# Feed-forward products: one PSUM tile of two banks becomes two tiles of one bank

## The chip, the core and the metric

The kernel runs on one core of a Trainium2 chip. The metric is device time in microseconds of one execution. The engines have short names here: PE is the matrix engine (its weight loads are shown apart, as PEld), DVE the vector engine, ACT the scalar engine, POOL the GpSimd engine and SP the engine that issues most of the transfers. Every engine works through its own list of instructions in order; semaphores make one engine wait for another. PSUM is the memory that PE writes its products to; here it is used as 8 banks of 512 float32 values on each of 128 partitions.

## The reference

```
q_pool = q.reshape(B, H, S // 2, 2, D).mean(axis=3)         # B 4, H 8, S 1152, D 64
scores = (q_pool @ k.T) / sqrt(D);  attn = softmax(scores)
x = (attn @ v), heads side by side                            # 2304 x 512
h = x @ w_in                                                  # 2304 x 2048
g = h * tanh(softplus(h))                                     # Mish
out = g @ w_out                                               # 2304 x 512, float32
```

The first half is an attention with pooled queries, the second a feed-forward layer with Mish between two matrix products. The change touches the second half alone.

## The kernel before

The attention fills the first part of the program and leaves its result transposed in SBUF, in `xT`. The feed-forward layer then works on three blocks of 768 tokens (`tp` 0, 1, 2), and in each on pairs of 128-wide slices of the hidden dimension (`fp` 0 to 7). One pair (block, slice pair) is a unit, written `(tp, fp)`; names in the trace carry no such numbers. Both matrix products are done by a seven-product (Winograd form of Strassen) scheme, and each float32 product as three passes over rounded parts: high by high, high by low, low by high. So one product of the scheme is a few groups of three matmuls of 128x384.

In a unit, `HP` (line 616 of the profile) makes the seven products of the first matrix, 42 matmuls, into PSUM tiles `ma`, `mb`, `mc` of a pool of their own. DVE and ACT combine them and apply Mish, and ACT and POOL split the results into high and low parts (`Gh`, `Gl`, `GhT`, `GlT`).

`OP(u, i, m)` (line 679) makes product `i` (1 to 7) of the second matrix for half `m` (0 or 1) of 128 output rows each: 14 groups of three matmuls, 42 in all. Products 1, 6, 7 and 4 form a chain: each is added in PSUM to what the one before left there. They share the tile `OA`, which is allocated once per unit as `[P, 2, 512]`, two banks, where half `m` uses bank `m`. After each step of the chain `EO(u, i, m)` (line 692, on DVE; in the first units of a block on ACT, line 690) adds the sum of that moment to the output in `xT`. Products 5, 3 and 2 use one-bank tiles with tags `x` (half 0) and `pv` (half 1).

In block 0 most units use a plain product, `OT` (line 732, groups of six matmuls of 128x512), whose six results are evicted by `EV` (line 740). Results 0 and 1, and 3 and 4, share a two-bank tile with the tag `Mb`; results 2 and 5 use `pv`. The last unit uses `OZ` (line 711) and `EZ` (line 716), with one bank of `Mb`, `x` and `pv` in turn. The tag `x` also holds a step of the weight conversion, `conv` (line 359).

The order in which each engine gets its instructions is written out by hand: tables of times (`FILL`, `EDGE`, `STEADY`) are sorted and issued in that order. No scheduler moves anything. What the tile framework adds are the waits: it tracks which tile an instruction reads or writes, and gives an instruction a semaphore wait where a tile's earlier reader or writer is on another engine.

Of the kernel before, what the change touches and what calls it, by code (L numbers as in the profile page):

```python
# [8 lines left out]
F32 = mybir.dt.float32  # L9
# [6 lines left out]
PSUM = bass.MemoryType.PSUM  # L16


def f32(ap):
    return ap.bitcast(F32)  # L20
# [3 lines left out]
def tile_pooled_attention_then_winograd_ffn(ctx: ExitStack, tc: tile.TileContext, q, k, v, moe_w_in, moe_w_out, out, outT):  # L24
# [3 lines left out]
    NT, DM = B * SQ, out.shape[1]  # L28
    DFF = moe_w_out.shape[0]
    P = 128  # L30
# [13 lines left out]
    TH = TW // 2  # L44
# [16 lines left out]
    pools, shut = {}, {}  # L61

    def open_pool(name, bufs, side="left", space=bass.MemoryType.SB):
        shut[name] = ExitStack()
        pools[name] = shut[name].enter_context(
            tc.tile_pool(name=name, bufs=bufs, side=side, space=space, reuse_waits="tile")
        )
        return pools[name]
# [3 lines left out]
    if True:  # L72
# [16 lines left out]
        dram = open_pool("dram", 1, space=bass.MemoryType.DRAM)  # L89
# [11 lines left out]
        ps1 = open_pool("ps1", 1, side="right", space=PSUM)  # L101
# [209 lines left out]
        wraw, wt, cw, cl, ws = {}, {}, {}, {}, {}  # L311
        wS, wO, wf = {}, {}, {}
# [24 lines left out]
        def conv(n, m):  # L337

            f, io = pieces[n]
            x = wraw[n]  # L340
            if n not in wt:
                wt[n] = wraw_p.tile([P, DM], F32, tag="wt", name=f"wt{n}") if n < 4 else w32((0, n // 4), n % 4)
            if n < 4 and 0 < m < 4:
                z = wt[n].bitcast(U16).rearrange("p (m two) -> p m two", two=2)
                u = x.bitcast(U16)
                if m == 1:
                    act.activation(z[:, :, 0], u[:, :, 1], AF.Copy, bias=2.0**-14 - 0.5, scale=2.0**-13)
                elif m == 2:
                    pool.tensor_scalar(z[:, :, 1], u[:, :, 3], 32768.0, 32768.0, ALU.is_ge, ALU.mult)
                else:  # L350
                    w = wt[n].bitcast(I32)
                    dve.scalar_tensor_tensor(
                        w, in0=cw[n].bitcast(I32), scalar=3, in1=w, op0=ALU.logical_shift_left, op1=ALU.bitwise_or
                    )
                return
            if n > 7:
                w, a = wt[n].bitcast(I32), x[:, :, 1]
                if m == 0:
                    cw[n] = ps1.tile([P, DM], F32, tag="x", name=f"cw{n}")
                    act.activation(cw[n], f32(a), AF.Copy, scale=2.0**-112)  # L360
                elif m == 1:
                    cl[n] = pools["psW"].tile([P, DM], I32, tag="cl", name=f"cl{n}")
                    act.activation(cl[n], x.bitcast(U16)[:, :, 1], AF.Copy, bias=2.0**-14 - 0.5, scale=2.0**-13)
                elif m == 2:
                    dve.scalar_tensor_tensor(w, in0=a, scalar=-(2**31), in1=cl[n], op0=ALU.bitwise_and, op1=ALU.bitwise_or)
                else:
                    dve.scalar_tensor_tensor(
                        w, in0=cw[n].bitcast(I32), scalar=3, in1=w, op0=ALU.logical_shift_left, op1=ALU.bitwise_or
                    )
                    load_w(n + 2)  # L370
                    sp.dma_start(out=spill[n], in_=wt[n])
                return
            if m == 0:
                cw[n] = wt[n] if n > 3 else ps1.tile([P, DM], F32, tag="x", name=f"cw{n}")
                act.activation(cw[n], f32(x[:, :, 1]), AF.Copy, scale=2.0**-112)
                return
            w = cw[n].bitcast(I32)
            if m == 1:
                dve.tensor_scalar(w, w, 3, None, ALU.logical_shift_left)
            elif m == 2:  # L380
                dve.scalar_tensor_tensor(
                    w, in0=x[:, :, 1], scalar=-(2**31), in1=w, op0=ALU.bitwise_and, op1=ALU.bitwise_or
                )
            elif m == 3:
                dve.scalar_tensor_tensor(
                    wt[n].bitcast(I32), in0=x[:, :, 0], scalar=29, in1=w, op0=ALU.logical_shift_right, op1=ALU.bitwise_or
                )
                load_w(n + 2)
                sp.dma_start(out=spill[n], in_=wt[n])
            elif m == 4:  # L390
                ws[f, io] = [pools["w0"].tile([P, DM], F32R, tag=f"{t}{io}{f}", name=f"w{t}{io}_{f}") for t in "hl"]
                act.copy(ws[f, io][0], wt[n])
                sp.dma_start(out=spill[n], in_=wt[n])
            else:
                hi, lo = ws[f, io]
                pool.tensor_tensor(lo, wt[n], f32(hi), ALU.subtract)
# [23 lines left out]
        hs, gs, os_, ch = {}, {}, {}, {}  # L420
# [243 lines left out]
        CHAIN_O = (1, 6, 7, 4)  # L664

        def OP(u, i, m):
            q, s, g = PROD[i]
            wh, wl = (x[:, s, m * P:(m + 1) * P] for x in weights(u, q))
            gh, gl = gs[u, g]
            if i == 1 and m == 0:  # L670
                o = ps1.tile([P, 2, 512], F32, tag="Mb", name=f"OA{u[0]}_{u[1]}")
                os_[u, "A"] = o[:, :, 0:TH]
            if i in CHAIN_O:
                o = os_[u, "A"][:, m]
            else:
                o = ps1.tile([P, 512], F32, tag=("x", "pv")[m], name=f"O{i}{m}_{u[0]}_{u[1]}")[:, 0:TH]
                os_[u, i, m] = o
            for n, (x, y) in enumerate(((wh, gh), (wh, gl), (wl, gh))):
                pe.matmul(o, x, y, start=(n == 0 and i not in CHAIN_O[1:]), stop=(n == 2 and i not in CHAIN_O[:3]), skip_group_check=True)  # L679

        def EO(u, i, m):
            tp, fp = u
            first = u in FIRST
            if i == 5 and first:
                ex[tp, m] = pools["wq"].tile([P, TH], F32, tag=f"ex{m}", name=f"ex{m}_{tp}")
            h, t = {1: (0, 0), 2: (0, 0), 6: (0, 1), 3: (0, 1), 7: (1, 1), 4: (1, 0), 5: (0, 0)}[i]
            acc = ex[tp, m] if i == 5 else half(tp, h, t)[:, m]
            o = os_[u, "A"][:, m] if i in CHAIN_O else os_[u, i, m]
            if first and (i == 5 or tp == 2 and i in (1, 6, 7, 4)):
                act.copy(acc, o)  # L690
            else:
                dve.tensor_tensor(acc, acc, o, ALU.add)  # L692
# [8 lines left out]

        def OZ(u, n):
            t, c = 1 - n // NKC, n % NKC
            o = ps1.tile([P, 2, 512], F32, tag="Mb", name=f"OZ{n}")[:, 0, 0:TH] if n % 3 == 0 else ps1.tile([P, 512], F32, tag=("x", "pv")[n % 3 - 1], name=f"OZ{n}")[:, 0:TH]
            os_[u, n] = o
            wh, wl = wf[u, "o"]
            for f in range(2):
                g, l = gs[u, 2 * f + t]
                a, b = (w[:, f, c * P:(c + 1) * P] for w in (wh, wl))
                for m, (x, y) in enumerate(((a, g), (a, l), (b, g))):  # L710
                    pe.matmul(o, x, y, start=(f == 0 and m == 0), stop=(f == 1 and m == 2))  # L711
# [6 lines left out]

        def OT(u, n):
            k = (n + KT // 2) % KT  # L720
            if n % 3 == 0:
                o = ps1.tile([P, 2, 512], F32, tag="Mb", name=f"O{u[0]}_{u[1]}_{n}")
                os_[u, n], os_[u, n + 1] = o[:, 0], o[:, 1]
            elif n % 3 == 2:
                os_[u, n] = ps1.tile([P, 512], F32, tag="pv", name=f"O{u[0]}_{u[1]}_{n}")
            o = os_[u, n]
            t, a = divmod(k, KT // 2)
            wh, wl = wf[u, "o"]
            for f in range(2):
                g, l = (x[:, a * P:(a + 1) * P] for x in gs[u, 2 * f + t])  # L730
                for m, (x, y) in enumerate(((g, wh), (g, wl), (l, wh))):
                    pe.matmul(o, x, y[:, f], start=(f == 0 and m == 0), stop=(f == 1 and m == 2))
# [15 lines left out]
        for n, u in enumerate(units):  # L748
            if u[0] == 0:
                banks[u] = ("b", "a", "c") if n % 2 else ("a", "b", "c")  # L750
            else:
                x, y, z = banks[units[n - 1]]
# [6 lines left out]
        def close(*names):  # L759
            for n in names:  # L760
                shut[n].close()
# [9 lines left out]
        def reuse_psH():  # L771
            close("psH")
            open_pool("psW", 1, space=PSUM)

        def reuse_rest():
            close("p3", "p2", "p1")
# [7 lines left out]
        def reuse_lead():  # L784
# [604 lines left out]
            (load_q, -3.5700),  # L1389
        ]  # L1390
        EDGE = [
            (-191.5356, split_h, 1, 1),
            (-182.6058, split_l, 1, 1),
            (-166.9356, split_h, 1, 2),
# [1181 lines left out]
        for _, fn, *a in plan:  # L2576
            fn(*a)
        mode.close()
        close("wq", "g", "sx", "ev", "xt", "pad", "wf", "xp", "wraw", "psW", "ps1", "dram")


SHAPE = (4, 8, 1152, 64)
# [34 lines left out]
```

## Time and profile before

| what | value |
| --- | --- |
| median of 3 runs | 815.39 us (813.95 to 815.86) |
| the profiled execution | 815.27 us, span of its instructions 813.2 us |
| PE busy | 774.7 us, 95% of the span |
| DVE, ACT, POOL busy | 686.3, 642.7, 652.1 us |
| granted PE clock | 0.996 of full speed over the span |

The profiled execution is 0.1 us from the median, and 2.1 us longer than the span of its instructions. Times in rows count from the start of the span. The attention ends and block 0 of the feed-forward layer begins near 455 us; blocks 1 and 2 run from about 570 us to the end. A matmul is shown for 0.34 us when it is 384 columns wide, and the next one starts about 0.17 us after it, so that back to back matmuls overlap in the picture; the idle time in square brackets counts from the end of the one before, and what a stall costs is longer than that idle time by the overlap.

### The profile page before, as it was taken

The page shows a single profiled execution, that of the slowest core. Times are in us where ns is not written, and L with a number is a line of the kernel's source. Part 1 is how long each engine was busy: PE and PEld are TensorE (multiplying, and loading weights), DVE is VectorE, ACT ScalarE, POOL GpSimd, SP SyncE. Part 2 cuts the span into 40 slices and gives each one's busy share as a digit, 9 for nine tenths or more (in the row PEclk, how much of TensorE's full clock was granted, in tenths as well). Part 3 has the DMA queues.
Part 4 walks back from the last instruction along what each step waited for, and adds up shares of the span by engine and source line. Part 5 has one row for each costly group of instructions (what it writes and reads, how often), then busy time and mean ns, then how long its engine had stood idle before and what let it go on. Part 6 is the DMA issues. An engine that isn't in the chain of part 4 may idle for free. (4 is left out here: it accounts for less than half of the span.)

```text
span 813.2 us, 14323 instructions
## 1 busy us (share of the span) xinstructions
PE 774.7 (95%) x5123; PEld 554.9 (68%) x5123; DVE 686.3 (84%) x959; ACT 642.7 (79%) x1110; POOL 652.1 (80%) x505
## 2 busy tenths in 40 slices
PE   6999999999999999999899999999989999899988
PEld 4455455555555554554569888997989989799987
DVE  5999999999999999999858688876677797567666
ACT  6999999999999999999768887776765676765752
POOL 4779998898898898898983987777776788777883
PEclk9999999999999999999999999999999999999999
DMA  7557546546656556555426887856543221433322
GB/s 266 154 157 186 144 133 174 120 135 144 164 141 170 116 138 146 139 139 115 85 50 193 284 287 245 271 174 189 172 160 110 91 92 49 132 112 107 116 98 97
DMA packets 44470, 121.90 MB, mean 150 GB/s; under 512 B 4592, under 2 KB 16368, under 8 KB 44400
## 3 DMA queue, kind: packets, MB, share of 16 engines
q1 hardware_dynamic: 34608, 71.45, 26.6%
q0 software_dynamic: 4608, 28.31, 17.7%
q10 hardware_dynamic: 5184, 21.24, 7.7%
q8 instruction: 40, 0.66, 0.3%
q14 instruction: 30, 0.25, 0.1%
HBM read 70.65 MB, written 22.02 MB: 114 GB/s over the span
## 5 line engine op out<-in xcount | busy, mean ns | idle before, releaser
L164 PE MATMUL s<-qT,kT 64*128 64x288 f32 x1152 | 202.5, 448 | 5.7 <-ACT TA L174 2.9
L164 PEld LDWEIGHTS s<-qT,kT 64*128 64x128 f32 x1152 | 91.8, 186 | 101.1 <-DVE rmax L185 25.4
L174 ACT COPY TA<-s 128x576 f32<-128x576 f32 x192 | 117.7, 638 | 22.4 <-PE s L164 16.0
L223 DVE TENSOR_TENSOR TA<-TA,Mb 128x1152 f32<-128x1152 f32 x96 | 128.9, 1348 | 1.7 <-PE Mb L217 0.8
L246 PE MATMUL pv<-TA,vn 128*64 128x288 f32 x768 | 116.5, 426 | 1.1 <-ACT TA L227 1.1
L227 ACT ACTIVATE TA<-TA 128x1152 f32<-128x1152 f32 x96 | 112.8, 1176 | 4.2 <-DVE TA L223 3.8
L232 POOL TENSOR_TENSOR acc<-TA 128x1152 f32<-128x1152 f32 x32 | 85.1, 2661 | 35.9 <-PE s L164 19.0
L238 POOL TENSOR_TENSOR acc<-acc 128x576 f32<-128x576 f32 x64 | 92.1, 1439 | 3.8 <-DMA acc<-TB 2.6
L185 DVE TENSOR_TENSOR rmax<-s,rmax 128x576 f32<-128x576 f32 x128 | 93.4, 750 | 1.4 <-ACT TB L174 1.2
L246 PEld LDWEIGHTS pv<-TA,vn 128*64 128x64 f32 x768 | 47.7, 138 | 48.8 <-issue 10.5
L692 DVE TENSOR_TENSOR xT<-xT,OA 128x384 f32<-128x384 f32 x104 | 55.0, 550 | 28.0 <-PE OA L679 27.9
L223 DVE TENSOR_TENSOR TB<-TB,Mb 128x1728 f32<-128x1728 f32 x32 | 62.2, 1945 | 0.0
L246 PE MATMUL pv<-TB,vn 128*64 128x288 f32 x384 | 61.3, 415 | 0.0
L174 ACT COPY TB<-s 128x576 f32<-128x576 f32 x96 | 59.8, 654 | 0.8 <-PE s L164 0.8
L598 POOL TENSOR_TENSOR wbl<-wS,wbh 128x1024 fp32r<-128x1024 f32 x20 | 49.6, 2481 | 8.8 <-ACT wbh L594 8.8
L227 ACT ACTIVATE TB<-TB 128x1728 f32<-128x1728 f32 x32 | 52.7, 1648 | 0.0
L185 DVE TENSOR_TENSOR rmax<-s,TA 128x576 f32<-128x576 f32 x64 | 48.4, 756 | 4.2 <-ACT TA L174 4.1
L598 POOL TENSOR_TENSOR wal<-wS,wah 128x768 fp32r<-128x768 f32 x19 | 35.7, 1878 | 19.6 <-ACT wah L594 19.4
L234 POOL TENSOR_TENSOR acc<-TA 128x576 f32<-128x576 f32 x32 | 45.6, 1426 | 1.8 <-ACT TA L227 1.7
L246 PEld LDWEIGHTS pv<-TB,vn 128*64 128x64 f32 x384 | 23.9, 136 | 25.2 <-issue 11.9
L598 POOL TENSOR_TENSOR woal<-wO,woah 128x1024 fp32r<-128x1024 f32 x13 | 31.4, 2417 | 9.8 <-ACT woah L594 8.8
L620 ACT COPY s<-ma 128x384 f32<-128x384 f32 x44 | 21.2, 482 | 20.4 <-PE ma L616 20.4
(305 smaller groups left out, 2246.0 us busy)
## 6 DMA issues: line engine op xcount, KB each, us to landing
acc<-TB POOLq DMA_DIRECT2D x32, 864.0 KB, 6.4
ri<-in_moe_w_in_dram SPq DMA_DIRECT2D x16, 512.0 KB, 4.3
ro<-in_moe_w_out_dram SPq DMA_DIRECT2D x16, 512.0 KB, 4.7
qn<-in_q_dram ACTq DMA_DIRECT2D x12, 576.0 KB, 5.1
kT<-in_k_dram ACTq DMA_DIRECT2D x12, 576.0 KB, 3.8
vn<-in_v_dram ACTq DMA_DIRECT2D x12, 576.0 KB, 4.1
wS<-sumsh SPq DMA_DIRECT2D x12, 512.0 KB, 4.0
wO<-sumso SPq DMA_DIRECT2D x13, 384.0 KB, 4.2
```

The source lines that it names most:

```text
L164: pe.matmul(s[:, j, 0:HQ], kT[64 * j:64 * j + 64, c], qT[64 * j:64 * j + 64, hf], start=True, stop=True,)
L174: act.copy(T(i, c), ss[i, c])
L185: dve.tensor_tensor(ss[i, c] if c == FOLD else r, ss[i, c], x, ALU.max)
L223: dve.tensor_tensor(x, x, Mbs[i].unsqueeze(1).to_broadcast([P, w, W]), ALU.subtract)
L227: act.activation(x, x, AF.Exp, scale=0.0625)
L232: pool.tensor_tensor(accs[i][:, 0:2], T(i, 0, 2), T(i, 2, 4), ALU.add)
L234: pool.tensor_tensor(accs[i][:, 2], T(i, 4), T(i, 5), ALU.add)
L238: pool.tensor_tensor(accs[i][:, 0], accs[i][:, 0], accs[i][:, n - 2], ALU.add)
L246: pe.matmul(pvs[i][64 * j:64 * j + 64, 0:HQ], vn[:, j, c, :], T(i, c)[:, j], start=(pvn[i] == 1), stop=(pvn[i] == NC),)
L598: (dve if e == "dve" else pool).tensor_tensor(l, w_part(u, q), f32(h), ALU.subtract)
L620: act.copy(sv[u, n], ps[u, "c" if n == 2 else "a"])
L692: dve.tensor_tensor(acc, acc, o, ALU.add)
```

## The change

A second PSUM pool, `ps2`, takes the place of `ps1` in the feed-forward layer. It is opened where `ps1` is closed, in `reuse_ps1`, at a place of the `EDGE` table just before the first `OT` products. The two banks of the tag `Mb` become two tags of one bank, `y0` and `y1`; `x` and `pv` stay. Both pools have four banks, so nothing else moves. `OA` is now a list of two tiles, one for each half; `OT` takes `y0`, `y1` and `pv` in turn; `OZ` goes round all four tags where it used three.

```diff
-                o = ps1.tile([P, 2, 512], F32, tag="Mb", name=f"OA{u[0]}_{u[1]}")
-                os_[u, "A"] = o[:, :, 0:TH]
+                os_[u, "A"] = [pools["ps2"].tile([P, 512], F32, tag=t, name=f"OA{t}{u[0]}_{u[1]}")[:, 0:TH] for t in ("y0", "y1")]
             if i in CHAIN_O:
-                o = os_[u, "A"][:, m]
+                o = os_[u, "A"][m]
...
-            o = ps1.tile([P, 2, 512], F32, tag="Mb", name=f"OZ{n}")[:, 0, 0:TH] if n % 3 == 0 else ps1.tile([P, 512], F32, tag=("x", "pv")[n % 3 - 1], name=f"OZ{n}")[:, 0:TH]
+            o = pools["ps2"].tile([P, 512], F32, tag=("y0", "y1", "x", "pv")[n % 4], name=f"OZ{n}")[:, 0:TH]
...
-            if n % 3 == 0:
-                o = ps1.tile([P, 2, 512], F32, tag="Mb", name=f"O{u[0]}_{u[1]}_{n}")
-                os_[u, n], os_[u, n + 1] = o[:, 0], o[:, 1]
-            elif n % 3 == 2:
-                os_[u, n] = ps1.tile([P, 512], F32, tag="pv", name=f"O{u[0]}_{u[1]}_{n}")
+            os_[u, n] = pools["ps2"].tile([P, 512], F32, tag=("y0", "y1", "pv")[n % 3], name=f"O{u[0]}_{u[1]}_{n}")
...
+        def reuse_ps1():
+            close("ps1")
+            open_pool("ps2", 1, side="right", space=PSUM)
...
+            (47.9700, reuse_ps1),
```

The instructions of each engine, and their order, are those of before; what differs is which of them wait, and for what. On DVE in unit (1, 3), before, these are the evictions of product 1, half 0 and half 1, the two instructions behind them, and the evictions of product 6, which share a row because they read alike:

```order
L692 TENSOR_TENSOR xT_60<-xT_60,OA1_3_6762 128x384 [waits DVE_49,PE_49]
L692 TENSOR_TENSOR xT_60<-xT_60,OA1_3_6762 128x384 [waits DVE_49]
L653 TENSOR_TENSOR T4f1_3_6786<-ma1_3_6518,T2f1_3_6719 128x384 [waits Activation_49]
L692 TENSOR_TENSOR ex0_1_6055<-ex0_1_6055,O50_1_3_6780 128x384 [waits PE_49]
L692 TENSOR_TENSOR xT_60<-xT_60,OA1_3_6762 128x384 [waits PE_49] x2
```

The same place with the change:

```order
L691 TENSOR_TENSOR xT_60<-xT_60,OAy01_3_6784 128x384 [waits DVE_49,PE_49]
L691 TENSOR_TENSOR xT_60<-xT_60,OAy11_3_6785 128x384 [waits DVE_49,PE_49]
L653 TENSOR_TENSOR T4f1_3_6809<-ma1_3_6539,T2f1_3_6741 128x384 [waits Activation_49]
L691 TENSOR_TENSOR ex0_1_6074<-ex0_1_6074,O50_1_3_6803 128x384 [waits PE_49]
L691 TENSOR_TENSOR xT_60<-xT_60,OAy01_3_6784 128x384 [waits PE_49]
L691 TENSOR_TENSOR xT_60<-xT_60,OAy11_3_6785 128x384 [waits PE_49]
```

Nothing moved. Before, the second eviction has no wait for PE of its own: the first one already waits until PE has written both halves of the tile. With the change each of the two waits for its own half.

On PE in the same unit, before, these are the two groups of product 7 (half 0, then half 1), which add to the bank that product 6 left:

```order
L679 MATMUL OA1_3_6762<-GhT31_3_6733,woah1_3_6683 128x384 [waits DVE_49]
L679 MATMUL OA1_3_6762<-GlT31_3_6734,woah1_3_6683 128x384 [waits Pool_49]
L679 MATMUL OA1_3_6762<-GhT31_3_6733,woal1_3_6684 128x384
L679 MATMUL OA1_3_6762<-GhT31_3_6733,woah1_3_6683 128x384
L679 MATMUL OA1_3_6762<-GlT31_3_6734,woah1_3_6683 128x384
L679 MATMUL OA1_3_6762<-GhT31_3_6733,woal1_3_6684 128x384
```

The same six with the change:

```order
L678 MATMUL OAy01_3_6784<-GhT31_3_6755,woah1_3_6705 128x384 [waits DVE_49]
L678 MATMUL OAy01_3_6784<-GlT31_3_6756,woah1_3_6705 128x384 [waits Pool_49]
L678 MATMUL OAy01_3_6784<-GhT31_3_6755,woal1_3_6706 128x384
L678 MATMUL OAy11_3_6785<-GhT31_3_6755,woah1_3_6705 128x384 [waits DVE_49]
L678 MATMUL OAy11_3_6785<-GlT31_3_6756,woah1_3_6705 128x384
L678 MATMUL OAy11_3_6785<-GhT31_3_6755,woal1_3_6706 128x384
```

Here too the instructions are the same. Before, the first group waits for DVE once, for the evictions of both halves that stand ahead of it in the program, and the second needs no wait of its own. With the change each half waits for its own bank's eviction.

## Rows read from the trace of the kernel before

**Rows 1.** The page, busy time and its share of the span, by engine
```profile
PE 774.7 (95%) x5123; PEld 554.9 (68%) x5123; DVE 686.3 (84%) x959; ACT 642.7 (79%) x1110; POOL 652.1 (80%) x505
```
**Rows 2.** Busy time by stretch, columns named in its first row
```profile
core 0: us, PE busy (x) PEld busy (x) DVE busy (x) ACT busy (x) POOL busy (x), PEclk, DMA share, GB/s
500.00:560.00 60.00, 59.65 (x297) 53.05 (x295) 47.68 (x75) 43.95 (x83) 47.40 (x39) 1.00 0.69 224
560.00:620.00 60.00, 54.95 (x300) 52.03 (x300) 41.94 (x83) 36.68 (x71) 44.53 (x28) 1.00 0.48 152
620.00:700.00 80.00, 73.86 (x409) 69.99 (x409) 60.74 (x113) 54.54 (x110) 63.49 (x44) 1.00 0.28 93
700.00:780.00 80.00, 73.36 (x409) 70.04 (x408) 56.42 (x116) 51.08 (x102) 63.45 (x43) 1.00 0.36 116
...
638.65:655.05 16.40, 15.07 (x85) 14.47 (x85) 12.62 (x25) 11.47 (x24) 13.52 (x10) 1.00 0.41 132
```
**Rows 3.** Groups of PE instructions, 560 to 814 us, that were waited before
```profile
line engine op names shapes xcount | busy us, mean ns | idle before us <-releasers
...
L679 PE MATMUL OA<-GhT,woah 128*128 128x384 f32 x56 | 21.4, 382 | 15.2 <-DVE xT L692 14.4 <-ACT xT L690 0.6
...
L616 PE MATMUL ma<-T4h,wbh 128*128 128x384 f32 x30 | 10.2, 340 | 0.6 <-DVE mb L624 0.6
...
L732 PE MATMUL O<-woh,Gh 128*128 128x512 f32 x8 | 3.3, 407 | 1.6 <-DVE xT L740 1.6
```
**Rows 4.** Everything on tile OA: durations (min/median/max), and who waited for it
```profile
L692 DVE TENSOR_TENSOR xT<-xT,OA x104: 541/548/555, 574.2 to 799.9; 128x384 f32<-128x384 f32 x104
...
  PE OA L679: 15.6, 23
```
**Rows 5.** Timeline of PE and DVE in unit (1, 3), 638.65 to 642.74 us
```profile
638.65 0.34 PE L679 MATMUL OA<-Gh,woah 128*128 128x384 f32 x1
...
639.52 0.34 PE L679 MATMUL OA<-Gh,woal 128*128 128x384 f32 x1
639.69 0.34 PE L679 MATMUL O<-GhT,woah 128*128 128x384 f32 x1
...
639.89 1.02 DVE L692 TENSOR_TENSOR xT<-xT,OA 128x384 f32<-128x384 f32 x2 [1.46 <-PE OA L679]
640.04 0.34 PE L679 MATMUL O<-GhT,woal 128*128 128x384 f32 x1
...
641.06 0.41 PE L679 MATMUL OA<-GhT,woah 128*128 128x384 f32 x1 [0.68 <-DVE xT L692]
...
641.30 0.33 PE L679 MATMUL OA<-GlT,woah 128*128 128x384 f32 x1
641.47 0.34 PE L679 MATMUL OA<-GhT,woal 128*128 128x384 f32 x1
641.85 0.56 DVE L692 TENSOR_TENSOR xT<-xT,OA 128x384 f32<-128x384 f32 x1
642.46 0.44 PE L679 MATMUL OA<-GhT,woah 128*128 128x384 f32 x1 [0.65 <-DVE xT L692]
642.74 0.34 PE L679 MATMUL OA<-GlT,woah 128*128 128x384 f32 x1
```
**Rows 6.** Timeline of PE, first products of unit (0, 7) held back
```profile
559.37 0.33 PE L616 MATMUL mc<-T1h,wbl 128*128 128x384 f32 x1
561.33 0.50 PE L732 MATMUL O<-woh,Gh 128*128 128x512 f32 x1 [1.64 <-DVE xT L740]
```
**Rows 7.** Timeline of POOL and PE: the weights that are used soonest after they are made
```profile
651.04 2.42 POOL L598 TENSOR_TENSOR wbl<-wS,wbh 128x1024 fp32r<-128x1024 f32 x1
...
654.36 0.34 PE L616 MATMUL mc<-T1h,wbl 128*128 128x384 f32 x1
```
**Rows 8.** Timeline of DVE, full-width operations on SBUF
```profile
645.32 0.95 DVE L509 TENSOR_TENSOR T4f<-xT,T2f 128x768 f32<-128x768 f32 x1
...
654.46 1.78 DVE L509 TENSOR_TENSOR T3f<-xT 128x768 f32<-128x768 f32 x1
```

More of the change, by code (lines that the diff above doesn't have):

```diff
@@ L358, in conv @@
                 if m == 0:
-                    cw[n] = ps1.tile([P, DM], F32, tag="x", name=f"cw{n}")
+                    cw[n] = pools.get("ps2", ps1).tile([P, DM], F32, tag="x", name=f"cw{n}")
                     act.activation(cw[n], f32(a), AF.Copy, scale=2.0**-112)
@@ L670, in OP @@
             if i == 1 and m == 0:
-                o = ps1.tile([P, 2, 512], F32, tag="Mb", name=f"OA{u[0]}_{u[1]}")
-                os_[u, "A"] = o[:, :, 0:TH]
+                os_[u, "A"] = [pools["ps2"].tile([P, 512], F32, tag=t, name=f"OA{t}{u[0]}_{u[1]}")[:, 0:TH] for t in ("y0", "y1")]
             if i in CHAIN_O:
-                o = os_[u, "A"][:, m]
+                o = os_[u, "A"][m]
             else:
-                o = ps1.tile([P, 512], F32, tag=("x", "pv")[m], name=f"O{i}{m}_{u[0]}_{u[1]}")[:, 0:TH]
+                o = pools["ps2"].tile([P, 512], F32, tag=("x", "pv")[m], name=f"O{i}{m}_{u[0]}_{u[1]}")[:, 0:TH]
                 os_[u, i, m] = o
@@ L687, in EO @@
             acc = ex[tp, m] if i == 5 else half(tp, h, t)[:, m]
-            o = os_[u, "A"][:, m] if i in CHAIN_O else os_[u, i, m]
+            o = os_[u, "A"][m] if i in CHAIN_O else os_[u, i, m]
             if first and (i == 5 or tp == 2 and i in (1, 6, 7, 4)):
@@ L2578, in tile_pooled_attention_then_winograd_ffn @@
         mode.close()
-        close("wq", "g", "sx", "ev", "xt", "pad", "wf", "xp", "wraw", "psW", "ps1", "dram")
+        close("wq", "g", "sx", "ev", "xt", "pad", "wf", "xp", "wraw", "psW", "ps2", "dram")
 SHAPE = (4, 8, 1152, 64)
```

## The prediction, made before the changed kernel was run

> **What bounds the kernel now.** I read the busy time first: PE is busy 95% of the span, no other engine above 84% [rows 1]. An average hides the stages, so next comes the table by stretch. From 500 to 560 us, block 0 of the feed-forward layer, PE is busy 59.65 of 60 us: it sets the pace and has next to nothing to win. From 560 us on, in blocks 1 and 2, it falls to 54.95 of 60 and then 73.9 and 73.4 of 80 us, while DVE and POOL stay at 70 to 79% [rows 2]. PE is still the fullest engine there, yet it stops now and then; the question is for whom.
>
> The groups that were waited before answer it: of PE's idle time in 560 to 814 us, 15.2 us stand before the groups that add to `OA` (products 6 and 7), 14.4 of it ended by line 692, DVE's evictions, and 1.6 us before one `OT` group [rows 3]. The view of the tile has the same from the other side: PE waited 23 times for something that touched `OA`, 15.6 us in all [rows 4].
>
> The timeline of one unit shows how [rows 5]. Product 1 is written by PE from 638.65 (half 0) and 639.17 (half 1; its last matmul starts at 639.52). DVE has been idle for 1.46 us and starts both evictions only at 639.89, when both halves are there; they take 1.02 us together. Product 6, half 0, is then issued at 641.06, when both evictions are over. Its result is evicted at 641.85 to 642.41, and product 6, half 1, starts at 642.46, 0.05 us behind that eviction, although it writes the other bank, whose eviction ended at 640.91. The two banks are held together because they are one tile.
>
> **What the change removes.** Six matmuls in a row start 0.174 us apart ((640.04 - 638.65) / 8) [rows 5]. The first matmul of product 6 could have started at 640.04 + 0.17 = 640.21; it started at 641.06, a loss of 0.85. Half 1 could have followed at 641.47 + 0.17 = 641.64; it came at 642.46, a loss of 0.82. After each stall the second matmul comes late too: 0.24 and 0.28 us behind the first instead of 0.17, another 0.18. In all 1.85 us in this unit. A check: the unit lasts 16.40 us from one product 1 to the next [rows 2], and 84 matmuls (42 of each matrix) at 0.174 need 14.6, so 1.8 us are lost in it, and the two stalls are all of them.
>
> With a tile for each bank, the eviction of half 0 needs only half 0. The last matmul of that half starts 0.52 us (three matmuls) before that of half 1, so the eviction can start at 639.89 - 0.52 = 639.37. A single eviction takes 0.55 us [rows 4], so it is over at 639.92, before PE reaches product 6 at 640.21: no wait, with 0.29 us to spare. Half 1's eviction starts at 639.89 and is over at 640.44; product 6, half 1, is due at 640.21 + 3 x 0.174 = 640.73: again no wait, 0.29 us to spare. The wait behind product 6's own eviction is gone altogether. Products 7 and 4 come several groups later and were not held up here. So both stalls go.
>
> **The sum.** What a stall costs is its idle time in the profile, plus the 0.17 us by which the matmul before it overlaps, plus the late second matmul (0.18 / 2 = 0.09). For the tile `OA`: 15.6 + 23 x 0.26 = 21.6 us [rows 4]. One more stall belongs to the same cause: in unit (0, 7), `OT`'s result 1 shares a tile with result 0, whose eviction stands before it in the program; PE waits from 559.37 + 0.17 to 561.33, 1.8 us [rows 6], and with its own tile result 1 needs no eviction at all. Sum 23.4 us.
>
> Against it I set 1 us. Late in block 1 PE also waits for DVE at `ma<-T4h` (0.6 us, line 624) [rows 3], where DVE's own work is long: the full-width `T3f` takes 1.78 us there, the like-sized `T4f` ten microseconds earlier 0.95 [rows 8]. PE arrives earlier there after the change and DVE can't follow as fast, so that wait grows; I take one such operation's excess (0.83) and round up. The bounds of this term are 0 and some four such operations, 3.3 us.
>
> The rest is priced at nothing. The added waits and signals of PE (each half of a chain step now tells DVE of itself): the last matmul of product 1 ends a group for which DVE waits, and the next one follows 0.17 us later as everywhere else [rows 5]; between 0 and 1 us. The Trainium skill speaks against that: "TensorE: Matmul & The Clock Gate", "The cost: per-tile semaphore tail", gives 26.3 ns for every matmul that raises a semaphore, as such increments queue up behind one another. With at most 70 more of them (4 chain steps in 14 units, 2 pairs in 7 units of block 0) that would be an estimated 1.8 us, and the time 794.5; no row here shows such a tail. DVE's evictions beside PE's writes to the other bank: all 104 evictions of `OA` lie between 541 and 555 ns, whether PE was writing meanwhile or stood still [rows 4], so I expect no slower ones. The pool swap happens once, where both pools have four banks, and `OZ`'s fourth bank helps only if `OZ` waits for a bank, for which PE lost nothing that has a row in [rows 3].
>
> 815.3 (profiled) - 23.4 + 1.0 = 792.9; the median of the runs is 0.1 us from the profiled time. I forecast 792.5 us, 2.8% less, with a range of its own of 789 to 797: the upper end leaves the boundary term at 3.3 and the added signals at 1, the lower end takes both at 0 and lets DVE and ACT, which also start sooner, win another 2 us at the borders of the blocks.
>
> **Rivals.**
>
> *The next late operand takes part of it.* What PE needs soonest after it is made is POOL's `wbl`: made at 651.04 to 653.46, used at 654.36, 0.9 us to spare [rows 7]. POOL works 13.52 of the 16.40 us of a unit [rows 2]; in a unit of 14.6 it has 1.1 us of slack left, DVE 2.0. If POOL does not move forward with PE, the first 0.9 of the 1.85 us are kept and the rest is lost again as a wait for weights: 0.95 us in each of some 9 steady units, 8.6 us, time 801. For it speaks that POOL is in order and nearly full; against it, that POOL's own idle time comes from waiting for work that PE releases, so that it moves too. Chance 0.18.
>
> *The change does not do what it says.* If the stalls stemmed from something other than the shared tile, all stays: 815. By the Trainium skill ("Perfetto Trace Analysis", "Optimizing Tensor Performance") independent groups should rotate through different banks so that evacuation overlaps the next group; the two halves already did that before, and by this rule alone nothing would change. The row disagrees: half 1 starts 0.05 us behind an eviction of the other bank [rows 5]. Chance 0.05.
>
> *Slower.* PE becomes denser from 560 us on, and its granted clock could fall to the lower of its two levels (1.2 GHz of 2.4); that a matmul then takes twice as long is an estimate from the ratio of the two. The forecast is some 230 us for what lies behind 560 us; each microsecond of it that is granted only half costs half a microsecond of work. From 47 us at the lower level the gain is eaten up; 80 us of it would give 792.5 + 40 = 832. Against it: in 500 to 560 us PE was busy 99% and the granted clock was 1.00, the upper level [rows 2]. Chance 0.03.
>
> **Chances.** Forecast 0.74, part of it 0.18, no change 0.05, slower 0.03. The range that should hold the time is 788 to 803: it takes in the forecast's own range and the first rival. A measurement of this kernel can't tell less than about 0.2% (1.6 us) from no change; faster than that 0.92, within it 0.05, slower 0.03.
>
> **What would show it.** In the changed profile: a steady unit of 14.6 us instead of 16.40; PE's waits for DVE before the `OA` groups near zero; DVE's first eviction of a unit starting while PE is still writing half 1; 460 instead of 409 matmuls in 80 us of blocks 1 and 2. The boundary term is right if the wait at `ma<-T4h` is about 1 us longer. I am wrong if PE's waits at `OA` remain, if they turn up at `wbl` or `GlT` instead, or if the granted clock from 560 us on is below 1.00.

## The result and the profile after

The changed kernel takes 784.65 us (median of 4 runs, 782.86 to 786.41), the kernel before 815.05 (4 runs beside it). The ratio is 0.9628, with an interval of 0.9603 to 0.9653: a gain of 30 us, 3.7%. I had forecast 792.5 us with a range of 788 to 803. The direction was right and the gain a third larger than I said; the time lies below the range.

The page's first part after the change, to be held against [rows 1]: PE is busy 98% of a shorter span.

```profile
PE 767.4 (98%) x5123; PEld 558.1 (71%) x5123; DVE 680.6 (87%) x959; ACT 642.1 (82%) x1110; POOL 654.3 (84%) x505
```

By stretch, with the columns of [rows 2]; the last row is the steady unit from one product 1 to the next:

```profile
500.00:560.00 60.00, 59.96 (x298) 53.51 (x297) 47.70 (x75) 44.09 (x81) 47.57 (x38) 1.00 0.64 215
560.00:620.00 60.00, 60.00 (x341) 59.08 (x341) 47.56 (x94) 41.41 (x82) 51.18 (x33) 1.00 0.57 182
620.00:700.00 80.00, 80.00 (x462) 79.53 (x461) 64.98 (x129) 60.92 (x123) 73.76 (x47) 1.00 0.30 95
700.00:780.00 80.00, 79.30 (x458) 78.96 (x456) 62.53 (x128) 48.99 (x97) 64.62 (x46) 1.00 0.39 128
...
628.03:642.58 14.55, 14.55 (x85) 14.55 (x85) 12.62 (x25) 11.39 (x24) 13.55 (x10) 1.00 0.47 161
```

Where 80 us held 409 matmuls they hold 458 to 462, at the same granted clock of 1.00, and the unit lasts 14.55 us instead of 16.40. PE is never idle from 560 us to its last matmul, which ends at 779.30. The groups of [rows 3] after the change (the last column is idle time before them) show that not only the stalls at the products are gone, but also the wait at `ma<-T4h`, which I had expected to grow:

```profile
L678 PE MATMUL OAy<-GhT,woah 128*128 128x384 f32 x56 | 18.8, 336 | 0.0
L616 PE MATMUL ma<-T4h,wbh 128*128 128x384 f32 x30 | 10.1, 336 | 0.0
```

The view of the tile, against [rows 4], has the evictions as long as before, and for PE one wait of its weight loads is left:

```profile
L691 DVE TENSOR_TENSOR xT<-xT,OAy x104: 540/547/556, 570.0 to 769.5; 128x384 f32<-128x384 f32 x104
...
  PEld OAy L678: 0.2, 1
```

The timeline of unit (1, 3), PE and DVE, against [rows 5]:

```profile
628.03 0.34 PE L678 MATMUL OAy<-Gh,woah 128*128 128x384 f32 x1
...
628.75 1.07 DVE L691 TENSOR_TENSOR xT<-xT,OAy 128x384 f32<-128x384 f32 x2 [0.94 <-PE OAy L678]
...
629.42 0.34 PE L678 MATMUL O<-GhT,woal 128*128 128x384 f32 x1
629.59 0.34 PE L678 MATMUL OAy<-GhT,woah 128*128 128x384 f32 x1
...
630.11 0.34 PE L678 MATMUL OAy<-GhT,woah 128*128 128x384 f32 x1
```

DVE starts its first eviction 0.72 us after the product's first matmul; before it was 1.24 us (638.65 to 639.89). That is the 0.52 us that three matmuls take. Product 6 follows 0.17 us behind its neighbour, and its second half 0.52 us later. In unit (0, 7), result 1 no longer waits, against [rows 6]:

```profile
557.74 0.34 PE L616 MATMUL mc<-T1h,wbl 128*128 128x384 f32 x1
557.92 0.39 PE L727 MATMUL O<-woh,Gh 128*128 128x512 f32 x1
```

### The profile page after: what moved, and what is told of

Its sections match the earlier page's. It is cut to its first block, busy times and chain, and to the rows that moved or that the text cites. A ratio compares the mean times of both kernels' runs of the same rounds, so it can differ in the third digit from the quotient of the medians.

```text
span 782.7 us, 14324 instructions
## 1 busy us (share of the span) xinstructions
PE 767.4 (98%) x5123; PEld 558.1 (71%) x5123; DVE 680.6 (87%) x959; ACT 642.1 (82%) x1110; POOL 654.3 (84%) x505
## 4 chain that ended last, share of the span: by engine, by line
PE 86%; DVE 3%; ACT 3%; DMA 3%; POOL 2%; issue 1%; SPq 0%; ACTq 0%; DVEq 0%; POOLq 0%
PE s L164 20%; PE pv L246 17%; PE ma L616 11%; PE O L727 8%; PE OAy L678 7%; PE mc L616 6%; PE O L678 6%; PE mb L616 3%; PE Sb L268 2%; DMA acc<-TB 2%; PE mt L200 2%; PE h L433 1%; PE Mb L217 1%; PE OZ L710 1%; POOL acc L238 1%
## 5 line engine op out<-in xcount | busy, mean ns | idle before, releaser
L164 PE MATMUL s<-qT,kT 64*128 64x288 f32 x1152 | 205.4, 454 | 4.0 <-ACT TB L174 1.8
L164 PEld LDWEIGHTS s<-qT,kT 64*128 64x128 f32 x1152 | 94.0, 189 | 99.8 <-DVE rmax L185 24.9
L691 DVE TENSOR_TENSOR xT<-xT,OAy 128x384 f32<-128x384 f32 x104 | 54.7, 548 | 11.9 <-PE OAy L678 11.6
```

Source lines behind the costliest of these rows:

```text
L164: pe.matmul(s[:, j, 0:HQ], kT[64 * j:64 * j + 64, c], qT[64 * j:64 * j + 64, hf], start=True, stop=True,)
```

## Where the gain comes from, counted from start to start

A sum over "idle before" is too small for two reasons, and both can be seen in the trace of the kernel before. The first is that the profile puts the end of a matmul later than the start of the next one (0.34 us long, 0.17 us apart), so of each gap only what exceeds this overlap is idle time, and of a short one too little to be noted. Here one product waits between its neighbours, and no bracket says so:

```profile
673.69 0.34 PE L679 MATMUL O<-GhT,woal 128*128 128x384 f32 x1
674.13 0.42 PE L679 MATMUL OA<-GhT,woah 128*128 128x384 f32 x1
674.39 0.34 PE L679 MATMUL OA<-GlT,woah 128*128 128x384 f32 x1
```

From start to start it is 0.44 + 0.26 instead of 0.17 + 0.17: 0.35 us lost, with 0.10 us of idle time (674.13 - 674.03). There are 29 such stalls at `OA`, not 23. Five of the six that I had missed are as short as this one; the sixth, at 571.78, is ended by the eviction of a result of block 0 that lay in the same two banks (line 740). From start to start, with the late second matmul, the 29 come to 23.9 us, where I had 21.6.

The second is that PE had other waits before, small ones, which don't stand at `OA`'s tile and are gone as well. These are the two largest, the first with the matmul ahead of it:

```profile
492.94 0.40 PE L732 MATMUL O<-woh,Gl 128*128 128x512 f32 x1
494.70 0.44 PE L616 MATMUL mb<-xhp,wah 128*128 128x384 f32 x1 [1.36 <-DVE Gl L637]
...
789.09 0.44 PE L679 MATMUL O<-GhT,woah 128*128 128x384 f32 x1 [1.11 <-DVE xT L692]
```

To see both sides without the attention before them, I take two lengths from each trace: from the first matmul of `OT` to the first of `OA` (block 0), and from there to the end of the last matmul (blocks 1 and 2). The first three columns are the times of these places.

| kernel | first `OT` | first `OA` | end of last matmul | block 0, us | blocks 1 and 2, us |
|---|---|---|---|---|---|
| before | 456.58 | 571.78 | 809.73 | 115.20 | 237.95 |
| after | 456.58 | 567.67 | 779.30 | 111.09 | 211.62 |
| difference | | | | 4.11 | 26.33 |

Block 0: the stall at `OT` (1.90), the wait at 494.70 (1.63, of it 0.11 at the late second matmul) and the first matmul of the very first `OA` (0.58) make 4.11. Blocks 1 and 2: the other 28 stalls (23.2) and the vanished waits at 666.05, 669.59, 699.50 and 789.09 (0.91 + 0.41 + 0.43 + 1.38 = 3.1) make 26.3 of 26.33. (The expectation of e1 below has 23.7 for the 29 stalls and 3.2 for these four waits.) So the whole gain has names. What needed experiments is why the other waits went too.

## Experiments

**Theory and rival.** My theory after the result (collision theory): DVE's full-width instructions with both operands in SBUF and POOL's instructions exclude each other, so that whoever starts later waits. Their order turns over with shifts of half a microsecond, and those waits of PE were collisions that the changed kernel happens to escape. The rival (queue theory): DVE works in order, its queue was held at each first eviction until the second half was there, and everything behind it was late by that. The two don't exclude each other, as it turned out.

**e1: the products of blocks 1 and 2 alone.** The results of block 0 keep the paired tile, and `OZ` stays on three tags. The edit against the kernel before, cut:

```diff
-                o = ps1.tile([P, 2, 512], F32, tag="Mb", name=f"OA{u[0]}_{u[1]}")
-                os_[u, "A"] = o[:, :, 0:TH]
+                os_[u, "A"] = [pools["ps2"].tile([P, 512], F32, tag=t, name=f"OA{t}{u[0]}_{u[1]}")[:, 0:TH] for t in ("y0", "y1")]
...
+            (157.6762, reuse_ps1),
```

> The change for the products OA of token blocks 1 and 2 alone; the results OT of block 0 keep the paired tile. Three accounts of the gain from 815.0 us. Forecast ledger (21.6 of stalls, less 1.0 for a longer wait elsewhere): 794.4. All 29 stalls of the products counted from start to start of neighbouring multiplies (23.7) and nothing else: 791.3. Those stalls and the four waits of TensorE for VectorE or GpSimd in block 1 that the trace after no longer has (0.99 at 666.05, 0.42 at 669.59, 0.43 at 699.50, 1.35 at 789.09, together 3.2): 788.1. In the last case no TensorE wait over 0.3 us stands after the block's first 10 us; in the other two those four are still there.

Measured: 787.32 us, ratio 0.9663 (0.9636 to 0.9689). First `OT` and `OA`, and last matmul:

```profile
458.06 0.39 PE L731 MATMUL O<-woh,Gh 128*128 128x512 f32 x1
572.53 0.34 PE L678 MATMUL OAy<-Gh,woah 128*128 128x384 f32 x1
783.80 0.34 PE L710 MATMUL OZ<-Gh,wol 128*128 128x384 f32 x1
```

Blocks 1 and 2 take 783.80 + 0.34 - 572.53 = 211.61, the same as in the changed kernel; block 0 takes 114.47, with the wait at `mb<-xhp` still there (1.22 us idle). The third account holds: the waits for DVE and POOL in blocks 1 and 2 went with the stalls of `OA`, nothing else of the change was needed.

**e2: the results of block 0 alone.** Blocks 1 and 2 keep the paired tile. The edit against the kernel before, cut to its added lines:

```diff
+            os_[u, n] = pools["ps2"].tile([P, 512], F32, tag=("y0", "y1", "pv")[n % 3], name=f"O{u[0]}_{u[1]}_{n}")
...
+                o = pools["ps3"].tile([P, 2, 512], F32, tag="Mb", name=f"OA{u[0]}_{u[1]}")
...
+            (47.9700, reuse_ps1),
+            (157.6762, reuse_ps2),
```

> The change for the results OT of token block 0 alone; blocks 1 and 2 keep the paired tile. If only the named stall at 561.33 (1.89 us) goes: 813.1. If the wait of 1.5 us at 494.70, where the first products of a tile wait for VectorE's Gl, goes with it as in the changed kernel: 811.6. The stalls of the products in blocks 1 and 2 stay: TensorE waits some 15 us or more for VectorE on OA.

Measured: 811.21 us, ratio 0.9957 (0.9939 to 0.9976). The same three places:

```profile
453.88 0.40 PE L728 MATMUL O<-woh,Gh 128*128 128x512 f32 x1
565.25 0.34 PE L679 MATMUL OA<-Gh,woah 128*128 128x384 f32 x1
802.76 0.34 PE L711 MATMUL OZ<-Gh,wol 128*128 128x384 f32 x1
```

Block 0 takes 111.37 (after: 111.09), blocks 1 and 2 take 237.85 (before: 237.95), and PE waits 15.6 us for `OA` as before. The two parts of the change add up: 0.9663 x 0.9957 = 0.9621, measured together 0.9628.

**e3: the last results on three tags.** The changed kernel without the fourth bank for `OZ`.

```diff
-            o = pools["ps2"].tile([P, 512], F32, tag=("y0", "y1", "x", "pv")[n % 4], name=f"OZ{n}")[:, 0:TH]
+            o = pools["ps2"].tile([P, 512], F32, tag=("y0", "x", "pv")[n % 3], name=f"OZ{n}")[:, 0:TH]
```

> The changed kernel with the last results OZ on three banks in turn instead of four. If the fourth bank for them is worth nothing, as TensorE has no stall in that stretch: 784.7, the same as the changed kernel within 0.2%. If the fourth bank carries part of the unforecast gain of 8 us: 786 or more, with TensorE waiting for an eviction in the last 15 us.

Measured: 783.73 us, ratio 0.9634 (0.9605 to 0.9663). Blocks 1 and 2 take 211.62 us, as with four: the fourth bank is worth nothing that can be measured.

**e4: the paired tile, its eviction issued one step later.** One line of the table of the kernel before is moved.

```diff
                 (18.9879, OP, 6, 0),
-                (19.3524, EO, 6, 0),
                 (19.4855, TG, "T4"),
                 (19.6516, OP, 6, 1),
+                (19.6517, EO, 6, 0),
```

> The kernel before with its paired tile; only in the ten steady units the step that evicts the first product of the second pair comes behind the step that issues the second product, in program order. If the stall is there because the tile of two banks is followed as one thing (the write of bank two is ordered behind the read of bank one that stands ahead of it in the program), one of the two stalls of each unit goes, 8 full ones of about 0.9 us: 808, with waits of TensorE for OA about halved. If VectorE or a bank itself were the limit, the stall would stay: 815.

Measured: 805.18 us, ratio 0.9891 (0.9865 to 0.9917); blocks 1 and 2 take 230.63 us, 7.3 less than before. The two profiled executions differ by 7.1 us (815.27 and 808.13), the medians of the runs by 9.9; the edit touches blocks 1 and 2 alone, so the 7.3 is the figure to read. PE's waits for `OA` fall from 23 (15.6 us) to 15 (9.8 us). PE in a steady unit, against [rows 5]:

```profile
638.43 0.41 PE L679 MATMUL OA<-GhT,woah 128*128 128x384 f32 x1 [0.68 <-DVE xT L692]
...
638.86 0.33 PE L679 MATMUL OA<-GhT,woal 128*128 128x384 f32 x1
639.03 0.33 PE L679 MATMUL OA<-GhT,woah 128*128 128x384 f32 x1
```

The first stall stays, the second is gone: with the same banks and the same DVE, half 1 follows at 0.17 us once the program no longer has an eviction between the two halves. So it is the program's order on one tile that made the stall, not a bank and not DVE's speed. That the first stall comes from the pair as well (DVE begins only when both halves are there) is shown by e1 and the change itself, where it goes. The price is that DVE now evicts both halves of product 6 only when both are there.

**p1: the two engines alone and side by side.** A program of subtractions only (lines 39 and 43 on DVE, 41, 45 and 51 on POOL; 48 and 53 on DVE with one operand in PSUM).

> No part of the task is computed: only subtractions on VectorE and GpSimd on tiles in SBUF, alone and side by side. Collision theory: VectorE's 128x768 with both operands in SBUF takes 0.95 us alone, and while GpSimd runs its own 128x768 (1.8 us) back to back many of VectorE's take 2 us or more, the sum of both engines' work being about the length of the stretch; VectorE's 128x384 with one operand in PSUM stays at 0.55 us beside the same GpSimd work. Without such a collision each keeps its time alone in all stretches.

Its groups (busy time, then the mean ns of one; 39 and 41 ran alone, 43 beside 45, 53 beside 51 but for its last four):

```profile
L45 POOL TENSOR_TENSOR p<-c,p 128x768 f32<-128x768 f32 x20 | 48.1, 2404 | 1.6
L43 DVE TENSOR_TENSOR v<-a,p 128x768 f32<-128x768 f32 x20 | 47.3, 2365 | 19.5 <-POOL p L41 18.8
L51 POOL TENSOR_TENSOR p<-c,p 128x768 f32<-128x768 f32 x10 | 18.1, 1808 | 0.8
L41 POOL TENSOR_TENSOR p<-c,v 128x768 f32<-128x768 f32 x10 | 18.0, 1799 | 14.2 <-DVE v L39 13.5
L53 DVE TENSOR_TENSOR v<-p,x 128x384 f32<-128x384 f32 x30 | 16.6, 553 | 1.0
L39 DVE TENSOR_TENSOR v<-a,b 128x768 f32<-128x768 f32 x10 | 9.5, 952 | 0.3
```

Side by side, both engines take turns: one instruction of each every 2.48 us from start to start (20 in 49.56), where they need 0.98 and 1.87 alone (10 in 9.83 and 10 in 18.70); the blocked one is shown as a long one. With one operand in PSUM, DVE takes 553 ns beside POOL, the last four without it 553 to 555, and POOL keeps its 1.81 us. The Trainium skill says in "SBUF — State Buffer", section "Who interferes with whom", that a DVE instruction with two SBUF inputs contends with a GpSimd instruction that reads SBUF, and calls the shared port pair an exclusive lock. The trace agrees in kind; in size, 0.98 + 1.87 would be 2.85 us, and 2.48 were measured, so some 0.37 us of each pair still overlap.

**e5 and e6: the order of one collision turned over.** T1f stands one instruction earlier in the kernel before, and one later in the changed kernel.

```diff
-            (84.2242, XS, 1, "T1"),
+            (83.4000, XS, 1, "T1"),
```

```diff
-            (84.2242, XS, 1, "T1"),
+            (85.4900, XS, 1, "T1"),
```

> The kernel before; on VectorE the subtraction T1f of the pair that follows (128x768, both operands in SBUF, 2.54 us at 487.96) stands one instruction earlier, and so starts before GpSimd's wal (487.83). Collision theory (such an instruction and one of GpSimd's exclude each other, and the one that starts later waits): T1f takes about 0.95 instead of 2.54 us, wal up to 0.6 us longer, VectorE's queue behind runs 1.5 us earlier, and TensorE's wait of 1.5 us at the first mb product (494.70) shrinks below 0.3: 813.5. Queue theory (VectorE was late because its queue had been held at evictions): T1f stays long or the wait stays, 815.0.

> The changed kernel; on VectorE T1f (0.95 us at 487.49) stands one instruction later, behind an eviction, and so starts after GpSimd's wal (487.69). Collision theory: T1f takes 2.0 to 2.5 us, wal 1.85 instead of 2.47, and a TensorE wait of 0.5 to 1.5 us is back at the first mb product near 493: 785.2 to 786.2. Queue theory: T1f about 1 us, no wait there, 784.7.

Measured: e5 814.55 us, ratio 1.0004 (0.9989 to 1.0019); e6 785.54 us, ratio 0.9644 (0.9618 to 0.9670). Both times alone tell nothing; the rows do. By time and wait e5 missed the collision theory's forecast (813.5 us, a wait below 0.3) and came out nearer to the queue theory's (815.0, the wait stays); the rows say why. First e5 (DVE, POOL and PE), then e6:

```profile
486.24 0.95 DVE L509 TENSOR_TENSOR T1f<-xT 128x768 f32<-128x768 f32 x1
...
488.90 3.19 DVE L509 TENSOR_TENSOR T2f<-xT,T1f 128x768 f32<-128x768 f32 x1
...
488.85 2.42 POOL L598 TENSOR_TENSOR wbl<-wS,wbh 128x1024 fp32r<-128x1024 f32 x1
...
493.21 0.44 PE L616 MATMUL mb<-xhp,wah 128*128 128x384 f32 x1 [1.00 <-DVE Gl L637]
```

```profile
487.56 2.27 DVE L509 TENSOR_TENSOR T1f<-xT 128x768 f32<-128x768 f32 x1
...
490.35 2.56 DVE L509 TENSOR_TENSOR T2f<-xT,T1f 128x768 f32<-128x768 f32 x1
...
494.03 0.45 PE L616 MATMUL mb<-xhp,wah 128*128 128x384 f32 x1 [1.32 <-DVE Gl L637]
```

T1f behaves as the collision theory said: 0.95 us when it starts ahead of POOL's `wal`, 2.27 when it starts behind. In e5 I missed what comes next: T2f now starts 0.05 us behind POOL's `wbl` and takes 3.19 us, so the gain of T1f is lost again in T2f. PE's wait goes with the two together (here the gap ahead of the waiting matmul alone, less the 0.23 us that its neighbour needs):

| kernel | T1f + T2f, us | PE held at `mb<-xhp`, us |
|---|---|---|
| e6 | 2.27 + 2.56 = 4.83 | 1.49 |
| before | 2.54 + 1.96 = 4.50 | 1.53 |
| e4 | 2.40 + 1.97 = 4.37 | 1.39 |
| e1 | 2.39 + 1.97 = 4.36 | 1.39 |
| e5 | 0.95 + 3.19 = 4.14 | 1.16 |
| after, e2 | 0.95 + 1.42 = 2.37 | 0 |

From before to e5 it is 0.36 us less work and 0.37 us less waiting, from before to e1 and e4 0.13 to 0.14 of each. In e6 the two take 0.33 us more than before and the wait is equal, since DVE comes to them 0.37 us earlier beside PE: its `Gl` ahead of them starts 6.41 us before PE's last matmul ahead of the wait (485.90 and 492.31), in the kernel before 6.04 us (486.90 and 492.94). e6's block 0 is 2.74 us longer than the changed kernel's; with the late second matmul this wait is 1.59, and the rest are three short waits ahead of the moved instruction (0.39, 0.28 and 0.48 at 464.85, 466.17 and 479.89), which the edit can't have caused.

**e7: the same in block 1 of the changed kernel.** T3f stands one instruction later.

```diff
-            (233.5708, XS, 2, "T3"),
+            (234.0500, XS, 2, "T3"),
```

> The changed kernel; in block 1 VectorE's T3f for the pair that follows (1.17 us at 641.76) stands one instruction later, behind an eviction of 0.54 us, and so starts after GpSimd's GlT (642.06). Collision theory: T3f takes 1.5 to 1.8 us, the instruction T1l that follows meets GpSimd's wobl and takes 2 us or more instead of 1.15, and with 0.5 us to spare at VectorE's mb (it ends at 650.91, TensorE needs it at 651.43) a TensorE wait of 0.5 to 1.5 us is back at ma<-T4h, as before at 666.05: about 785.7. Queue theory (those waits went because the evictions no longer held VectorE's queue): the same two instructions in the other order, all done at the same time, no wait, 784.7.

Measured: 787.44 us, ratio 0.9663 (0.9630 to 0.9695). The rows of the changed kernel first (DVE, then PE), then those of e7:

```profile
641.76 1.17 DVE L509 TENSOR_TENSOR T3f<-xT 128x768 f32<-128x768 f32 x1
...
646.28 1.15 DVE L521 TENSOR_TENSOR T1l<-T1f,T1h 128x768 fp32r<-128x768 f32 x1
...
648.95 1.02 DVE L521 TENSOR_TENSOR B21l<-xT,B21h 128x768 fp32r<-128x768 f32 x1
...
651.43 0.34 PE L616 MATMUL ma<-T4h,wbh 128*128 128x384 f32 x1
```

```profile
643.41 1.69 DVE L509 TENSOR_TENSOR T3f<-xT 128x768 f32<-128x768 f32 x1
...
647.92 2.50 DVE L521 TENSOR_TENSOR T1l<-T1f,T1h 128x768 fp32r<-128x768 f32 x1
...
651.75 2.17 DVE L521 TENSOR_TENSOR B21l<-xT,B21h 128x768 fp32r<-128x768 f32 x1
...
654.91 0.45 PE L616 MATMUL ma<-T4h,wbh 128*128 128x384 f32 x1 [1.16 <-DVE mb L624]
```

Two neighbouring instructions of DVE changed places, and three full-width ones became 3.0 us longer (1.69 + 2.50 + 2.17 against 1.17 + 1.15 + 1.02). The wait at `ma<-T4h` is back (1.43 us from start to start), the one at `mb<-B21h` behind it too (0.41), and evictions of `OA` stall PE for 0.45 and 0.54 us on the way; blocks 1 and 2 take 214.72 us instead of 211.62. I had expected about 1 us and got 3.1: B21l was one collision more than I had counted. The queue theory had expected no wait at all.

## Why the prediction was wrong in size

**Right.** Both stalls of a unit came from the shared tile, the unit became 14.55 us long (14.6 predicted), product 6 starts without a wait, and `OT` gave 1.90 us (1.8). e1 and e2 take the change apart and give the same; e4 shows the cause of the second stall itself. The fourth bank for `OZ` is worth nothing (e3).

**The step that failed.** "Against it I set 1 us": I let the wait at `ma<-T4h` grow, since DVE "can't follow as fast". It went to zero, and three more waits of blocks 1 and 2 went with it, together 3.1 us; e1 shows that splitting `OA` alone does that. I had seen the sign of it, T3f at 1.78 us beside T4f at 0.95 [rows 8], and read 0.83 us of excess as a property of the place. In e7 such an excess goes with POOL's instruction at that time (1.69 us behind it, 1.17 ahead of it), and nothing keeps that in place when everything moves by microseconds. The term should have had bounds on both sides; mine began at 0. (Of the 3.1 us, 1.38 turn out to be another thing, the wait at 789.09 below.) The same holds in block 0, where I named no wait to go: in the kernel before, T1f starts 0.13 us behind POOL's `wal` (487.96 and 487.83), after the change 0.20 us ahead of it (487.49 and 487.69), and 1.63 us of PE's wait at `mb<-xhp` go with that. e2 has T1f at 0.95 us and no wait, e1 has it at 2.39 us and the wait. The two rows before, then the two after:

```profile
487.96 2.54 DVE L509 TENSOR_TENSOR T1f<-xT 128x768 f32<-128x768 f32 x1
487.83 1.85 POOL L598 TENSOR_TENSOR wal<-wS,wah 128x768 fp32r<-128x768 f32 x1 [0.25 <-ACT wah L594]
...
487.49 0.95 DVE L509 TENSOR_TENSOR T1f<-xT 128x768 f32<-128x768 f32 x1
487.69 2.47 POOL L598 TENSOR_TENSOR wal<-wS,wah 128x768 fp32r<-128x768 f32 x1 [0.34 <-ACT wah L594]
```

What turned this order over is, by the rows, the shared tile too. Where results 0 and 1 share it and T1f stands in its old place (before, e1, e4), DVE stands idle for 0.22, 0.37 and 0.37 us before it evicts the two, 2.3 us ahead of T1f, and T1f starts 0.13, 0.28 and 0.27 us behind `wal`; in after, e2 and e3 it has no idle time there, and T1f starts 0.19 to 0.20 us ahead. So a queue held for 0.22 to 0.37 us decides the order, and the collision makes a wait of some 1.5 us of it. No run holds the queue alone, so this link is inferred.

**The term that was mis-sized.** The stalls of `OA`: 21.6 us by idle time plus 0.26 each, 23.9 us from start to start. Five stalls had too little idle time to be noted, and one was noted under another tile.

Both together, in us: 2.3 (short stalls) + 0.1 (`OT`) + 4.1 (the boundary term, from +1.0 to -3.1) + 1.6 (`mb<-xhp`) = 8.1, and 22.4 forecast + 8.1 = 30.5, where the two lengths above gave 30.44. (The prediction's own sum, 792.9, and the 792.5 that it states differ by 0.4 us, for which it has no term.)

**The rivals.** The next late operand did not come: `wbl` is ready at 641.13 and used at 641.90, 0.8 us to spare where there were 0.9; POOL is busy 13.55 of 14.55 us and still keeps up. The granted clock was 1.00 in every stretch shown, from 500 us on. The added signals cost nothing that shows: 84 matmuls in 14.55 us are 0.173 us each, as before.

**The wait at 789.09** (1.38 us) is no collision: there the rows of the kernel before show the held queue. PE waits to write a one-bank tile whose earlier result was complete at 786.42 (its last matmul starts at 786.08). In DVE's order that eviction stands behind the one of product 1, half 0, written from 785.22; and this one waited, with DVE idle, until half 1 was written too, whose last matmul starts at 787.64:

```profile
788.02 0.55 DVE L692 TENSOR_TENSOR xT<-xT,OA 128x384 f32<-128x384 f32 x1 [2.05 <-PE OA L679]
788.49 0.55 DVE L692 TENSOR_TENSOR xT<-xT,O 128x384 f32<-128x384 f32 x1
```

The eviction of the result ends at 789.04, and PE starts 0.05 us later. After the change DVE evicts half 0 at 758.67, the result at 759.14, and PE writes that tile at 760.41 without a wait. So this wait too was made by the shared tile, and the prediction had no term for it: it counted only PE's waits for `OA` itself, and not those for what stands behind `OA` in DVE's queue.

**What stays open.** That collisions bring back the waits at `ma<-T4h` and `mb<-B21h` is shown (e7); that they made them in the kernel before is inferred from the durations there (T3f 1.78, T1l 2.03, B21l 2.18 us against 1.17, 1.15 and 1.02 after). A held queue is unlikely at that place, since DVE's rows there have no idle time from 652.13 to the wait at 666.05. The 0.43 us at 699.50, a wait for POOL's `wal`, were not taken apart. None of the runs points to a version faster than the changed kernel: from 560 us on its PE has no stall left for such a turn to take away.

## What to carry to other kernels

Count what a stall costs from start to start of neighbouring matmuls, since idle time begins only where their overlap ends. A tile of two banks that is filled and emptied by halves is waited for as a whole, in the order of the program; look there first when an engine waits on a bank that has long been empty. When a change moves two engines against each other, waits that hang on the length of a contended instruction can vanish or come back, here by up to 1.6 us each: give that term bounds on both sides, and measure it by turning the order of one pair over. Count also what stands behind the held instruction in its engine's queue.

## What the runs showed that I had not expected

One place among DVE's instructions decides whether T1f takes 0.95 or 2.27 us, and a head start of 0.05 us is enough for POOL to make DVE's T2f last 3.19 us (e5), where one of its size takes 0.95 alone (p1). That is longer than POOL's whole instruction (2.42 us, of which 2.37 were left) by about the 0.82 us that DVE's own work then takes. And in e7 one swap of two neighbours costs 3.1 us, a tenth of what the whole change brought.
